# The last four 256-token blocks of a mixture layer as two blocks of 512 tokens, in a planned attention and MoE kernel

## The chip, the cores and the metric

One core of one Trainium2 chip runs the whole kernel. The metric is device time in microseconds (us) of one execution, as the median of several runs. The engines are named as the profile names them: PE is TensorE's matrix products, PEld its loading of the stationary operand, DVE VectorE, ACT ScalarE, POOL GpSimd, SP SyncE, which issues the transfers (DMA).

## The reference: what is computed

Causal attention over 4 sequences of 576 tokens with 8 heads of 64, mixed with a linear memory read by a gate per head; then two dense feed-forward layers, each with inner width 2048, over all 2304 tokens. Cut to what matters:

```python
local = softmax(causal(q @ k.T / 8)) @ v
x = g * mem_out + (1 - g) * local        # 2304 tokens x 512
h = x @ w_in;  x = (h * sigmoid(h)) @ w_out            # first MoE, weights 512x2048 and 2048x512
h = x @ w2_in; out = elu(h) @ w2_out                   # second MoE
```

The weights arrive as float64 and are turned into float32 on the chip.

## The kernel before

**Blocks.** The 2304 tokens are nine blocks of 256: A and B of each of the four sequences (query tiles 0 and 1; and two of the other three), and one block T that gathers the last 64 tokens of each sequence. `order` lists them as (0,A), (0,B), ... (3,B), (T,T), so `order[5]` is (2,B), `order[6:8]` are (3,A) and (3,B), and `order[8]` is T. Attention writes its results to DRAM (`xd`), and `x_load` fetches a block of it.

**First MoE.** `moe1_block` takes one block. For each pair j of 128-row tiles of the inner width it makes h (bank `h` of PSUM, two halves of 256 columns): per tile four slices of the depth, three products each, since every float32 is held as two float32r parts (upper by upper, upper by lower, lower by upper). That is 24 products of 256 columns for a pair. Then ACT takes tanh into `t`, DVE combines it with h, ACT and DVE split it into the two parts `g`, and 24 more products of 256 columns add the pair's share to `acc0` and `acc1`. A whole block has 8 pairs, so 192 + 192 = 384 products. For the first two blocks some pairs use float32 directly, and they are done in two halves; none of that is touched.

**Where it stands.** `interleave` mixes the attention of the later heads with blocks of `moe1` as filler for PE. The list `first` holds the halves of blocks 0 and 1 and `order[2:LAST]`, with LAST = 6, thus blocks 2 to 5. Blocks 6, 7 and T follow.

**Second MoE.** Pairs of its weight tiles are loaded (`w2_fetch`), turned to float32 (`w2_values`: one ACT and three DVE instructions for each of 4 tiles) and made into left operands (`w2_parts`). The raw tiles of pairs 0 and 1 have places of their own (`early`: x21 to x27 and g1, in pool `p2`, which opens when the attention pool is closed); later pairs are loaded into places (`stage`) of first weights that are done with, and so are all finished operands (`home`). Its second products are 512 columns wide already: operand `g` of 128 tokens stationary, 512 columns of the weight moving. Its first products are 256 wide.

**What sets the order.** Nothing runs in the order in which it is written. `Plan` collects all operations, `Plan.cost` gives each one a time, `Plan.schedule` makes a list schedule forwards and backwards four times, and the best one is emitted as a fixed order for every engine. For PE a single product of n columns was costed at

```python
return max(n / (2.4 if once else 0.6) + 2.0, 0.84 * m * (1 if once else 2))
```

nanoseconds, where `once` means float32r. All instructions are recorded through one helper (L194), so the profile's groups are told apart by tiles.

Of the kernel before, what the change touches and what calls it, by code (L numbers as in the profile page):

```python
# [27 lines left out]
AHEAD = 4  # L28
LAST = 6
W1A = 20  # L30
# [21 lines left out]
class View:  # L52
    """A part of a tile, named before the tile has its place on chip."""

# [59 lines left out]
    def box(self):  # L114
        """Partitions and columns that the view can touch (the whole bank in PSUM)."""
        t = self.tile
        if t.space == "psum":
            return (0, 128, 0, 1)
        lo = self.off
        hi = lo + sum(st * (n - 1) for st, n in self.dims)  # L120
        if t.space == "dram":
            return (0, 1, lo, hi + 1)
        w = t.width
        c = [(st, n) for st, n in self.dims if st % w]
        c0 = lo % w
        return (lo // w, hi // w + 1, c0, c0 + sum(st * (n - 1) for st, n in c) + 1)


class LateTile(View):
# [10 lines left out]
    def heads(self):  # L140
        """The operations that no other operation on the tile comes before."""
        users = set(self.users)
        return [o for o in users if not (o.deps & users)]
# [11 lines left out]
class Plan:  # L155
    """Collects the program, orders it by a list schedule over the engines, then emits it."""

# [27 lines left out]
    def add(self, eng, calls):  # L185
        """One operation: an instruction, or a few that an engine takes one after the other."""
        op = Op()
# [39 lines left out]
    def cost(op, fn, args, kw, ins, outs, together):  # L227
# [6 lines left out]
        if op.eng == "PE":  # L234
            if fn == "transpose":
                return max(ins[0].shape[0] / 1.2, 0.84 * cols(ins[0]))
            n, m, once = cols(kw["rhs"]), cols(kw["lhsT"]), kw["rhs"].dtype != F32
            if together > 1:
                return max(55.0, 30 + n / 4.8) if once else max(85.0, 27 + n / 1.2)
            return max(n / (2.4 if once else 0.6) + 2.0, 0.84 * m * (1 if once else 2))  # L240
        if op.eng == "DMA":
# [59 lines left out]
    def schedule(self, back):  # L301
        """List schedule: each engine takes, of what is ready, what comes first in priority.
        Backwards, it goes from the last operation to the first."""
        ops = self.ops
# [56 lines left out]
def attention_moe_moe_kernel(  # L361
# [50 lines left out]
    def mm2(parts):  # L412
        """Products on the two column halves of the array, side by side."""
        op = nc.add("tensor", [("matmul", (o,), dict(lhsT=l, rhs=r, start=start, stop=stop, skip_group_check=True))
                               for o, l, r, start, stop in parts])
        pe[0] += op.cost
# [7 lines left out]
    def split(t, src):  # L424
        """t[:, 0] and t[:, 1]: two float32r parts that add up to src."""
        split2(t[:, 0], t[:, 1], src)
# [33 lines left out]

    # Products that go nowhere, while the tensor engine would wait: they bring its clock up.
    zero = mask[:, 0:128]
# [4 lines left out]

# [1 line left out]
    win, wout = {}, {}  # L469
# [14 lines left out]

    # A float64 arrives as two 32-bit words. Scaling the upper word by 2^-112 as a float32
    # moves the exponent from bias 1023 to bias 127, for either sign; three bits of the lower
    # word complete the float32 significand. The value takes the place of the first half of the words.
    def w_value(raw):
# [41 lines left out]
    def w_again(c, f):  # L530
        """The parts of a weight tile that was used as a whole."""
        v = new(mp, [128, 512], F32, "t", 2)
# [3 lines left out]
    def part(w, i):  # L536
        """The upper (0) or lower (1) float32r part of a weight tile."""
        return w[:, (1 - i) * 512:(2 - i) * 512]

# [1 line left out]
    def x_load(blk):  # L541
        raw = new(mp, [128, 4, 256], F32, "stg", 2)
        b, r = blk
# [96 lines left out]

# [1 line left out]
    # Two heads at a time, which share the partitions: the first has 0..63, the second 64..127.  # L642
    bet = new(at, [128, H], F32, "sm4", 2)
# [16 lines left out]
    def native(task):  # L660
        """Scores from float32 operands, or from float32r parts (two passes, but parts to make)."""
        b, p, rg = task
        return b == 0 and p < (NATA if rg == "A" else NATB)
# [103 lines left out]
    def soft(task, u, nms):  # L767
        """Softmax, times 1 - g, of head u of the pair over the query tiles A (0 and 1) or 2 and 3,
        or of both heads over the last half tile."""
        b, p, rg = task  # L770
# [38 lines left out]
    def spread(t, c, u):  # L809
        """Of 128-column steps from c on, the half that is head u's."""  # L810
        return t[:, c:c + 256].rearrange("p (n h w) -> p n h w", h=2, w=64)[:, :, u, :]

    def a_T(task):
        """Probabilities of the query tiles 0 and 1, keys on the partitions, head by head."""
        res = []
# [10 lines left out]
    def b_T(task, kt):  # L826
        """The same of the query tiles 2, 4 and 3 for one tile of keys; 64 columns of one head are
        followed by 64 of the other."""
        a = new(at, [128, 640], F32, "a", 2)
# [53 lines left out]
    def av_mm(task, av, steps):  # L883
        """Adds to av (heads on either half of the partitions, queries along) for (columns, tile of
        keys, rows, probabilities of a head)."""
        v = pr_t[task]["v"]
# [66 lines left out]
    def merge(T, Sx):  # L953
        """The transposes and products of a pair between the softmax steps of the next one."""
        T, Sx = list(T), list(Sx)
# [85 lines left out]
    def place1(k):  # L1041
        """The places of the last weight tiles serve before those are there."""
        n = 2 * NF - LEND
# [19 lines left out]
    first = [x + (h,) for h in (0, 1) for x in order[:2]] + order[2:LAST]  # L1063
    g = moe1(first, order[LAST])
    calls = [0]
# [8 lines left out]

# [1 line left out]
    # Winograd's form of Strassen's seven products stands for the eight of h by halves: of the depth (k,  # L1076
    # two of its tiles each), of a pair of weight tiles (f) and of the tokens (n). With
    #   s1 = w01 + w11, s2 = s1 - w00, s3 = w01 - w00, s4 = w10 - s2,
    #   t1 = x01 - x00, t2 = x11 - t1, t3 = x01 - x11, t4 = x10 - t2 for w[k][f] and x[k][n]
    # they are w00 x00, w10 x10, s4 x11, w11 t4, s1 t1, s2 t2, s3 t3, and h[f][n] has h00 = p1 + p2,  # L1080
    # h01 = p1 + p6 + p5 + p3, h10 = p1 + p6 + p7 + p4, h11 = p1 + p6 + p7 + p5.
    # The pairs go over the tokens in two sweeps, whose sums meet in DRAM.
    nc.late[p2] = [o for row in nc.tags.values() for t in row if t.pool is at for o in t.users]
# [14 lines left out]

    # Places of the second weights, in the order in which the first ones are done with.
    slots = [f"w{c}_{2 * j + u}" for j in range(NF // 2) for c in range(2) for u in range(2)]  # L1100
# [10 lines left out]
    home["half", 3] = home["half", 0]  # L1111
    early = [(p2, f"x2{i}") for i in range(1, 8)] + [(p2, "g1")]
    w2t, wo2, w2raw, halves = {}, {}, {}, {}

    def w2_fetch(p):
# [3 lines left out]
        for i, (c, f) in enumerate(((0, 2 * p), (0, 2 * p + 1), (1, 2 * p), (1, 2 * p + 1))):  # L1119
            if p < 2:  # L1120
                pl, tag = early[4 * p + i]
                raw = new(pl, [128, 1024], I32, tag, 2 if tag == "g1" else 1)
            else:
# [8 lines left out]
    def w2_parts(p):  # L1132
        """The seven left operands of a pair of weight tiles, and its two tiles of the second product."""
        raws = w2raw.pop(p)
# [40 lines left out]
    def x2_split(raws):  # L1175
        """The right operands."""
        x = [[raw[:, 2 * k:2 * k + 2, :] for raw in raws] for k in range(2)]
# [23 lines left out]
    def product(p, o, wi, x, start, xi=None):  # L1201
        """Adds product wi to o."""
        n = 0
# [5 lines left out]
    def gemm1_2(p, x, nb):  # L1209
        """h, from the products of a pair."""  # L1210
        A, C = bank("s", 2), bank("tp", 2)
# [108 lines left out]
    def w2_steps(n, end):  # L1320
        """Steps of making the second weights, up to those of pair end - 1."""
        for _ in range(n):
# [3 lines left out]

    g = moe1(order[LAST:8], order[8])
    for p in range(2):
        w2_fetch(p)
    vals = [w2_values(p) for p in range(2)]  # L1330
    run(g)
    for p in range(2):
# [8 lines left out]

    run(moe1(order[8:], wnext=wnext))
    for x in parts:
# [81 lines left out]
```

## Time and profile before

| | |
|---|---|
| three runs | 1041.01, 1041.64, 1045.52 us; median 1041.64 us |
| span of the profiled execution | 1046.4 us |
| PE busy in the span | 1028.0 us, 98%, 7206 instructions |
| PEld, DVE, ACT busy | 87%, 68%, 60% |
| granted clock of PE, first 75 us; afterwards | 0.73 to 0.86; 1.00 |

The profiled execution's own span, 1046.4 us, is 4.8 us above the median of the runs. The page's busy time of PE is modelled from pipelined products, so a product's cost is read from starts: the start of one run of equal products to the start of the next, divided by their number.

### The profile page before, as it was taken

How to read it: one execution, taken by the hardware profiler on the slowest of the kernel's cores; microseconds unless marked ns; L12 is line 12 of the kernel's file. 1: busy time of each engine (PE TensorE's matmuls, PEld its weight loads, DVE VectorE, ACT ScalarE, POOL GpSimd, SP SyncE). 2: the span in 40 equal slices, each digit the busy share in tenths (PEclk: the TensorE clock that was granted, in tenths of full speed). 3: DMA queues.
4: the chain of work that ended last, by engine and by line, in shares of the span. 5: the costliest groups of instructions: out<-in, count | busy, mean ns of one | idle time of the engine just before them, and what ended most of it. 6: DMA issues, size and time to landing. Idle time of an engine off the chain costs nothing.

```text
span 1046.4 us, 19128 instructions
## 1 busy us (share of the span) xinstructions
PE 1028.0 (98%) x7206; PEld 913.2 (87%) x7206; DVE 715.5 (68%) x1782; ACT 632.9 (60%) x1434; POOL 9.9 (1%) x54
## 2 busy tenths in 40 slices
PE   7899999999999999999999999999999999999998
PEld 5456887998888888999999999999899899999997
DVE  4979998888777675552223257999969985656554
ACT  5878988989888787422223154766556654434333
POOL 1000000000000000000000000000000000000000
PEclk7889999999999999999999999999999999999999
DMA  8864673452433321601010013434225320302010
GB/s 243 285 168 129 162 228 102 120 168 78 143 98 95 116 86 34 230 10 41 1 41 21 1 42 117 145 105 143 69 91 174 106 100 22 101 22 81 21 61 21
DMA packets 102685, 105.19 MB, mean 101 GB/s; under 512 B 13760, under 2 KB 84928, under 8 KB 102592
## 3 DMA queue, kind: packets, MB, share of 16 engines
q1 hardware_dynamic: 102592, 103.97, 32.5%
q8 instruction: 56, 0.92, 0.4%
q14 instruction: 37, 0.30, 0.1%
HBM read 84.02 MB, written 19.92 MB: 99 GB/s over the span
## 4 chain that ended last, share of the span: by engine, by line
PE 94%; DVE 2%; DMA 2%; SPq 1%; issue 0%; ACT 0%; DVEq 0%
PE acc L194 31%; PE h L194 24%; PE s L194 16%; PE tp L194 13%; PE av L194 10%; SPq L194 1%; DVE w L194 1%; DMA w<-in_moe_w_out 1%; DMA kl<-in_kT 1%; DMA zb<-in_z_prev 0%; DVE e L194 0%; DVE qm L194 0%; DVE eA L194 0%; DVE sm L194 0%; DVE nm L194 0%
## 5 line engine op out<-in xcount | busy, mean ns | idle before, releaser
L194 PE MATMUL h<-x,w 128*128 128x256 f32 x1632 | 223.3, 286 | 0.0
L194 PE MATMUL acc<-g,w 128*128 128x256 f32 x1536 | 210.8, 286 | 0.0
L194 PEld LDWEIGHTS h<-x,w 128*128 128x128 f32 x1632 | 206.2, 191 | 1.9 <-issue 0.8
L194 PEld LDWEIGHTS acc<-g,w 128*128 128x128 f32 x1536 | 194.3, 191 | 0.9 <-issue 0.2
L194 PE MATMUL acc<-w,g 128*128 128x512 f32 x480 | 131.1, 392 | 0.0
L194 PE MATMUL s<-x,w 128*128 128x256 f32 x864 | 126.4, 282 | 0.0
L194 PEld LDWEIGHTS s<-x,w 128*128 128x128 f32 x864 | 118.3, 190 | 5.8
L194 DVE SCALAR_TENSOR_TENSOR t<-t,h 128x512 f32<-128x512 f32 x72 | 49.3, 685 | 107.9 <-ACT t L194 107.7
L194 ACT ACTIVATE e<-e,sm 128x512 f32<-128x512 f32 (+2 forms) x160 | 107.1, 687 | 14.8 <-DVE sm L194 14.6
L194 ACT ACTIVATE t<-h 128x512 f32<-128x512 f32 x72 | 43.0, 597 | 113.0 <-PE h L194 112.6
L194 PEld LDWEIGHTS acc<-w,g 128*128 128x128 f32 x480 | 85.8, 189 | 13.6
L194 PE MATMUL tp<-x,w 128*128 128x256 f32 x672 | 96.6, 282 | 0.0
L194 PEld LDWEIGHTS tp<-x,w 128*128 128x128 f32 x672 | 90.2, 190 | 3.4
L194 ACT COPY a<-tp 128x384 f32<-128x384 f32 (+2 forms) x160 | 65.1, 426 | 27.5 <-PE tp L194 21.0
L194 DVE SCALAR_TENSOR_TENSOR w<-w 128x512 int32<-128x512 int32 x108 | 72.4, 684 | 0.8 <-ACT w L194 0.3
L194 ACT ACTIVATE e<-h 128x512 f32<-128x512 f32 (+1 forms) x80 | 47.1, 590 | 39.4 <-DVE h L194 38.7
L194 DVE TENSOR_TENSOR g<-e,g 128x512 fp32r<-128x512 f32 (+1 forms) x80 | 50.5, 635 | 22.1 <-ACT g L194 21.1
L194 ACT CAST g<-e 128x512 fp32r<-128x512 f32 (+1 forms) x80 | 46.1, 578 | 26.1 <-DVE e L194 25.6
L194 DVE TENSOR_TENSOR g<-t,g 128x512 fp32r<-128x512 f32 x64 | 44.0, 688 | 24.3 <-ACT g L194 24.2
L194 DVE TENSOR_TENSOR x<-stg,x 128x256 fp32r<-128x256 f32 (+2 forms) x86 | 46.0, 550 | 20.4 <-ACT x L194 20.0
L194 PE MATMUL tp<-ident,e 128*128 128x128 f32 (+1 forms) x304 | 55.5, 280 | 4.4 <-ACT a L194 3.5
L194 PE MATMUL av<-a,vr 128*64 128x320 f32 (+4 forms) x448 | 59.1, 385 | 0.0
(137 smaller groups left out, 1611.2 us busy)
## 6 DMA issues: line engine op xcount, KB each, us to landing
w<-in_moe_w_in SPq DMA_DIRECT2D x27, 512.0 KB, 5.0
w<-in_moe_w_out SPq DMA_DIRECT2D x27, 512.0 KB, 4.7
raw<-in_kT SPq DMA_DIRECT2D x48, 144.0 KB, 2.9
y<-y SPq DMA_DIRECT2D x18, 256.0 KB, 2.6
qm<-in_qn SPq DMA_DIRECT2D x32, 128.0 KB, 2.4
vr<-in_vn SPq DMA_DIRECT2D x16, 256.0 KB, 2.9
raw<-in_qT SPq DMA_DIRECT2D x24, 144.0 KB, 3.1
raw<-in_qT SPq DMA_DIRECT2D x24, 128.0 KB, 2.7
```

The source lines that it names most:

```text
L194: r = getattr(issue, fn)(*[a.make() if isinstance(a, View) else a for a in args], **{k: v.make() if isinstance(v, View) else v for k, v in ...
```

## The change

`moe1_wide` takes two blocks at once: h of one tile of the inner width is one product chain of 512 columns into a bank of its own (two banks `s` and two banks `tp` in turn), `g` holds 512 tokens, and four whole banks (`acc0`, `acc1`, `h`, `av`) collect the result. It is called for blocks 6 and 7, and then for blocks 5 and T. LAST falls to 5, so block 5 is no longer among the filler of attention. The raw tiles of the second weights of pair 1 lose their own places and go to `stage`; pair 0 keeps four (x25, x26, x27, h2), the first two of which first hold the raw x of blocks 6 and 7. The cost that the planner puts on a product rises from n/2.4 + 2.0 to n/2.4 + 13.5 ns, which moves the whole order, attention included. The rest of the diff takes out comments.

```diff
-LAST = 6
+LAST = 5
...
-            return max(n / (2.4 if once else 0.6) + 2.0, 0.84 * m * (1 if once else 2))
+            return max(n / (2.4 if once else 0.6) + (13.5 if once else 3.0), 0.84 * m * (1 if once else 2))
...
+    def moe1_wide(blks, tags=(), wnext=None):
+        with nc.ahead(XHP):
+            raws = [x_load(blk, new(p2, [128, 4, 256], F32, tags[i]) if tags else None) for i, blk in enumerate(blks)]
+            x = []
+            for k in range(2):
+                hi, lo = [new(p2, [128, 2, 512], F32R, f"x2{2 * k + i + 1}") for i in range(2)]
+                for i, raw in enumerate(raws):
+                    c = slice(256 * i, 256 * i + 256)
+                    split2(hi[:, :, c], lo[:, :, c], raw[:, 2 * k:2 * k + 2, :])
+                x.append((hi, lo))
+        acc = [bank(tg) for tg in ("acc0", "acc1", "h", "av")]
+        g_t = {}
+
+        def gemm1(f):
+            h = bank(("s", "tp")[f % 2], 2)
+            w, n = win[f], 0
+            for kt in range(4):
+                c = slice(kt * 128, (kt + 1) * 128)
+                for wi, xi in ((0, 0), (0, 1), (1, 0)):
+                    mm(h[:], part(w, wi)[:, c], x[kt // 2][xi][:, kt % 2, :], n == 0, n == 11)
+                    n += 1
+            t = new(mp, [128, 512], F32, "t", 2)
+            g_t[f] = new(*((mp, [128, 2, 512], F32R, "g"), (p2, [128, 2, 512], F32R, "g1"))[f % 2], 2)
+            with nc.ahead(HP):
+                nc.scalar.activation(t[:], h[:], AF.Tanh, scale=0.5)
+                nc.vector.scalar_tensor_tensor(out=t[:], in0=t[:], scalar=1.0, in1=h[:], op0=ALU.add, op1=ALU.mult)
+                split(g_t[f], t[:])
+
+        def gemm2(f):
+            g, w = g_t.pop(f), wout[f]
+            for dm in range(4):
+                c = slice(dm * 128, (dm + 1) * 128)
+                for n, (wi, gi) in enumerate(((0, 0), (1, 0), (0, 1))):
+                    mm(acc[dm][:], part(w, wi)[:, c], g[:, gi, :], f == 0 and n == 0, f == NF - 1 and n == 2)
+
+        for f in range(NF + 2):
+            if f < NF:
+                gemm1(f)
+            if f > 1:
+                gemm2(f - 2)
+                if wnext is not None and f % 2:
+                    wnext(f // 2 - 1)
...
-    g = moe1(first, order[LAST])
+    g = moe1(first)
...
-    early = [(p2, f"x2{i}") for i in range(1, 8)] + [(p2, "g1")]
+    early = [(p2, t) for t in ("x25", "x26", "x27", "h2")]
...
-            if p < 2:
-                pl, tag = early[4 * p + i]
-                raw = new(pl, [128, 1024], I32, tag, 2 if tag == "g1" else 1)
+            if p == 0:
+                pl, tag = early[i]
+                raw = new(pl, [128, 1024], I32, tag)
...
-    g = moe1(order[LAST:8], order[8])
+    moe1_wide(order[6:8], ("x25", "x26"))
...
-    run(moe1(order[8:], wnext=wnext))
+    moe1_wide([order[5], order[8]], wnext=wnext)
```

What the planner made of it, at three places. In these names x is the split input (of narrow and wide blocks alike), w any weight tile (numbers cut short: w_10 is the tile of the tenth slice), g the split middle result.

TensorE in the first MoE after attention, one round before: the first products of two tiles for 256 tokens, then their second products.

```order
L194 MATMUL h_5840<-x_6_5705,w_2_1_2345 128x256 x3
L194 MATMUL h_5840<-x_6_5727,w_2_1_2345 128x256 x3
L194 MATMUL h_5840<-x_6_5731,w_2_1_2345 128x256 x3
L194 MATMUL h_5840<-x_6_5745,w_2_1_2345 128x256 x3
L194 MATMUL h_5840<-x_6_5705,w_3_1_2427 128x256 x3
L194 MATMUL h_5840<-x_6_5727,w_3_1_2427 128x256 x3
L194 MATMUL h_5840<-x_6_5731,w_3_1_2427 128x256 x3
L194 MATMUL h_5840<-x_6_5745,w_3_1_2427 128x256 x3
L194 MATMUL acc_8_5874<-g_5843,w_0_1_2677 128x256 x6
L194 MATMUL acc_8_5884<-g_5843,w_0_1_2677 128x256 x6
```

The same engine now, in the wide block of (3,A) and (3,B): the end of one tile's first products, then a tile's second products into four banks.

```order
L194 MATMUL s_6336<-x_0_5733,w_2_1_2366 128x512
L194 MATMUL s_6336<-x_0_5751,w_2_1_2366 128x512
L194 MATMUL s_6336<-x_0_5733,w_2_1_2366 128x512 x2
L194 MATMUL s_6336<-x_0_5751,w_2_1_2366 128x512
L194 MATMUL s_6336<-x_0_5733,w_2_1_2366 128x512
L194 MATMUL acc_9_6356<-g_6313,w_0_1_2648 128x512 x3
L194 MATMUL acc_9_6363<-g_6313,w_0_1_2648 128x512 x3
L194 MATMUL h_6369<-g_6313,w_0_1_2648 128x512 x3
L194 MATMUL av_6375<-g_6313,w_0_1_2648 128x512 x3
```

A product of width 512 stands where two of width 256 stood, and a tile's second products go to four banks instead of two.

TensorE at the end of attention before: the last products of the last heads (av), inside block (1,B) of the first MoE.

```order
L194 MATMUL acc_7_4862<-g_5628,w_13_0_1710 128x256 x5
L194 MATMUL av_5681<-a_5691,vr_5210 64x320 x2
L194 MATMUL av_5681<-a_5719,vr_5210 64x192 x2
L194 MATMUL av_5681<-a_5719,vr_5210 64x64 x2
L194 MATMUL av_5681<-pt_5712,ms_5543 128x320
L194 MATMUL acc_7_4862<-g_5628,w_13_0_1710 128x256
```

The same place now:

```order
L194 MATMUL h_5587<-x_5_4741,w_10_0_1354 128x256 x2
L194 MATMUL av_5544<-a_5556,vr_5075 64x320 x2
L194 MATMUL av_5544<-a_5585,vr_5075 64x192 x2
L194 MATMUL av_5544<-a_5585,vr_5075 64x64 x2
L194 MATMUL av_5544<-pt_5580,ms_5410 128x320
L194 MATMUL h_5587<-x_5_4741,w_10_0_1354 128x256
```

Attention now ends at the first products of tile 10 of that block, where before it ended at the second products of tile 13: counted over the whole order, 1184 products of the first MoE stand ahead of the last av row, 1313 before.

SyncE's transfers in the first microseconds before: the third pair of q and k (kh, kl) right behind the first two weight tiles.

```order
L194 DMA raw_161<-in_qT 64x576 x2
L194 DMA w_0_0_170<-in_moe_w_in 128x4x256
L194 DMA w_0_0_191<-in_moe_w_out 128x1024
L194 DMA kh_213<-in_qT 128x256
L194 DMA kl_223<-in_kT 128x256
```

And now:

```order
L194 DMA raw_163<-in_qT 64x576 x2
L194 DMA w_0_0_172<-in_moe_w_in 128x4x256
L194 DMA w_0_0_187<-in_moe_w_out 128x1024
L194 DMA zb_214<-in_z_prev 128x128
L194 DMA w_14_0_217<-in_moe_w_in 128x4x256
L194 DMA kh_246<-in_qT 128x256
L194 DMA kl_255<-in_kT 128x256
```

A small load and a third weight tile of 512 KB now stand ahead of that pair.

## Rows read from the trace of the kernel before

**Rows 1.** The page's head and its part 1: busy time, share, instructions.

```profile
span 1046.4 us, 19128 instructions
PE 1028.0 (98%) x7206; PEld 913.2 (87%) x7206; DVE 715.5 (68%) x1782; ACT 632.9 (60%) x1434; POOL 9.9 (1%) x54
```

**Rows 2.** Stretch, length; busy us (count) of PE, PEld, DVE, ACT, POOL; clock; DMA; GB/s.

```profile
0.00:25.00 25.00, 17.96 (x106) 12.13 (x107) 12.79 (x64) 13.46 (x40) 2.63 (x14) 0.73 0.83 249
25.00:50.00 25.00, 22.24 (x113) 11.89 (x111) 23.09 (x87) 21.32 (x58) 0.80 (x3) 0.86 0.86 278
...
75.00:175.00 100.00, 99.06 (x598) 75.63 (x596) 94.62 (x284) 87.24 (x217) 1.75 (x10) 1.00 0.55 158
175.00:250.00 75.00, 75.00 (x594) 67.07 (x593) 61.47 (x177) 68.29 (x167) 1.23 (x7) 1.00 0.45 130
250.00:425.00 175.00, 175.00 (x1363) 153.70 (x1362) 120.27 (x389) 140.35 (x352) 3.27 (x19) 1.00 0.31 91
...
450.00:625.00 175.00, 175.00 (x1461) 175.00 (x1460) 55.87 (x94) 49.66 (x92) 0.00 (x0) 1.00 0.08 22
...
700.00:850.00 150.00, 150.00 (x945) 135.83 (x944) 134.43 (x273) 94.53 (x192) 0.00 (x0) 1.00 0.33 108
```

**Rows 3.** Timeline of TensorE in the first MoE: start us, us, what, count.

```profile
434.77 3.04 PE L194 MATMUL acc<-g,w 128*128 128x256 f32 x24
437.65 3.04 PE L194 MATMUL h<-x,w 128*128 128x256 f32 x24
```

**Rows 4.** Timeline of TensorE in the second MoE, products 512 wide.

```profile
754.96 1.55 PE L194 MATMUL acc<-w,g 128*128 128x512 f32 x6
756.35 0.84 PE L194 MATMUL h<-w,g 128*128 128x512 f32 x3
...
1020.17 2.91 PE L194 MATMUL acc<-w,g 128*128 128x512 f32 x12
1022.91 1.12 PE L194 MATMUL tp<-x,w 128*128 128x256 f32 x8
...
1035.61 5.86 PE L194 MATMUL acc<-w,g 128*128 128x512 f32 x25
```

**Rows 5.** Groups of instructions of DVE and ACT: busy us, mean ns.

```profile
L194 DVE SCALAR_TENSOR_TENSOR w<-w 128x512 int32<-128x512 int32 x108 | 72.4, 684 | 0.8 <-ACT w L194 0.3
L194 DVE SCALAR_TENSOR_TENSOR t<-t,h 128x512 f32<-128x512 f32 x72 | 49.3, 685 | 107.9 <-ACT t L194 107.7
...
L194 DVE TENSOR_TENSOR g<-t,g 128x512 fp32r<-128x512 f32 x64 | 44.0, 688 | 24.3 <-ACT g L194 24.2
...
L194 ACT ACTIVATE t<-h 128x512 f32<-128x512 f32 x72 | 43.0, 597 | 113.0 <-PE h L194 112.6
...
L194 ACT CAST g<-t 128x512 fp32r<-128x512 f32 x64 | 39.6, 619 | 20.6 <-DVE t L194 20.6
...
L194 DVE TENSOR_SCALAR w<-w 128x512 int32<-128x512 int32 x54 | 22.3, 421 | 0.1
...
L194 DVE TENSOR_TENSOR h<-x,x 128x256 f32<-128x256 f32 x32 | 13.5, 421 | 8.9 <-ACT x L194 8.7
```

**Rows 6.** Timeline of all engines in the first 16 us.

```profile
8.47 0.51 SPq L194 DMA_DIRECT2D w<-in_moe_w_out  x1
...
9.50 0.61 SPq L194 DMA_DIRECT2D kl<-in_kT  x1
...
15.84 0.55 PE L194 MATMUL s<-kl,kh 64*128 64x128 f32 x1 [2.37 <-DMA kl<-in_kT]
```

**Rows 7.** Timeline at the end of attention.

```profile
424.67 0.81 PE L194 MATMUL av<-pt,ms 128*128 128x320 f32 x2
...
425.96 0.32 SPq L194 DMA_DIRECT2D xdB<-xt  x1
```

**Rows 8.** The page's part 6: KB of one load, us from issue to landing.

```profile
w<-in_moe_w_in SPq DMA_DIRECT2D x27, 512.0 KB, 5.0
```

**Rows 9.** Waits of TensorE from 75 to 430 us: total, times, longest.

```profile
PE tp L194 <- ACT a L194: 0.9, 1, 0.9
```

More of the change, by code (lines that the diff above doesn't have):

```diff
@@ L538, in part, with x_load @@
         return w[:, (1 - i) * 512:(2 - i) * 512]
-    def x_load(blk):
-        raw = new(mp, [128, 4, 256], F32, "stg", 2)
+    def x_load(blk, raw=None):
+        if raw is None:
+            raw = new(mp, [128, 4, 256], F32, "stg", 2)
         b, r = blk
@@ L639, in moe1_block @@
         nc.sync.dma_start(x2d[blk].rearrange("k p n -> p k n"), ev[:])
+    def moe1_wide(blks, tags=(), wnext=None):
[37 more added lines that the diff above has]
+                    wnext(f // 2 - 1)
+        for dm in range(4):
+            ev = new(mp, [128, 512], F32, "t", 2)
+            nc.scalar.activation(ev[:], acc[dm][:], AF.Copy, scale=0.5)
+            for i, blk in enumerate(blks):
+                nc.sync.dma_start(x2d[blk][dm], ev[:, 256 * i:256 * i + 256])
     bet = new(at, [128, H], F32, "sm4", 2)
@@ L1330, in attention_moe_moe_kernel @@
     vals = [w2_values(p) for p in range(2)]
-    run(g)
     for p in range(2):
```

## The prediction, made before the changed kernel was run

> **What bounds the kernel now.** I read the page's head first: PE is busy for 1028.0 of 1046.4 us [rows 1]. Since that busy time is modelled, the stretches come next. From 75 us on PE is busy for the whole of nearly every stretch at a granted clock of 1.00, the full 2.4 GHz, while DVE and ACT change from light to heavy [rows 2]. In the stretch of the last narrow blocks, 450 to 625 us, PE and PEld are both busy for 175 of 175 us, DVE for 56 and ACT for 50: nothing but the stream of products sets the pace there. In 700 to 850 us, the second MoE, DVE is busy for 134.4 of 150 us and PE still has no gap. Only the first 75 us are different: PE has 18 and 22 of 25 us, at clocks of 0.73 and 0.86, with the DMA engines busy for 83% and 86%. So a change after 425 us is worth what it takes off the stream of products, as long as it makes no new wait.
>
> **The products, the main term.** The timeline of the narrow stage starts 24 products at 434.77 us and the next 24 at 437.65 us [rows 3]: 2.88 us, 120.0 ns for 256 columns. The columns alone take 256 / 2.4 = 106.7 ns at that clock, which leaves 13.3 ns for each product. Four blocks of 384 are 1536 products, 1536 x 120.0 ns = 184.3 us. The change makes 768 of 512 columns. The first MoE has none today, but the second has, and its timeline gives three prices [rows 4]: six from 754.96 to 756.35 us, 231.7 ns each, with DVE heavily loaded; twelve from 1020.17 to 1022.91 us, 228.3 ns; and the last 25, 5.86 us with the last product's own 0.39 us in it, so 24 starts in 5.47 us, 227.9 ns. I take 228.3 ns, since DVE and ACT are light in the first MoE too: 768 x 228.3 = 175.3 us. **The term is -9.0 us.** Its ends: at 231.7 ns 177.9 us, -6.4; and if exactly half of the 13.3 ns goes away for every old product, 768 x 13.3 ns, -10.2.
>
> **Around the wide products, nothing.** Tanh, combining, cast and subtraction work on 128x512 before and after: 0.597 + 0.685 + 0.619 + 0.688 = 2.6 us in a chain [rows 5], 16 of them for two blocks as before. The chain of one tile is covered by 12 products of the next tile, 12 of the one after, and two sets of second products, 4 x 12 x 228.3 ns = 11.0 us; the narrow block has two sets of 24 x 120 ns, 5.8 us. If the chain came 8 us late in one place, PE would still not see it. The wide x of blocks (3,A) and (3,B) must come through DRAM from the last heads. In the order, 184 narrow products stand between the last av product and the end of the narrow round that precedes the first wide one, 22.1 us. The store is issued 1.3 us after the start of the last av product [rows 7], and even three transfers of 5.0 us each, the time of a 512 KB load [rows 8], with two pairs of cast and subtraction behind them are 1.3 + 15.0 + 2.6 = 18.9 us. Without that cover, if the wide block came first, it would be a gap of that size. Between the two wide blocks, and between the second one and the second MoE, 36 second products of 228.3 ns, 8.2 us, run while the next inputs are split: two casts and two subtractions of 512, 2.6 us, before the first of them is needed. I cost both seams at nothing.
>
> **The second weights.** Pair 1 loses its early place: its raw tiles wait for tiles 5 to 7 of the first weights, which are free only after about 11 of 32 sets of twelve in the last wide block, at 30 us of 88 us. Behind that, the order puts on DVE, up to the block's end, the values of 10 raw tiles (10 x (0.421 + 2 x 0.684) = 17.9 us), 9 steps of the block (9 x (0.685 + 0.688) = 12.4 us), 15 subtractions of full and 10 of half width (15 x 0.688 + 10 x 0.421 = 14.5 us): 44.8 us [rows 5]. It has from 30 + 5.0 us (the load) to about 84.5 us, 49.6 us, so it is loaded to 90%. The stretch of 700 to 850 us has DVE at the same 90% and PE without a gap [rows 2]. I take 0 and keep +3 as the upper end, one tile's values and one chain late at the last seam. It can't gain, because PE does not wait there today.
>
> **The start.** The third pair of q and k now stands behind one more small load and one more weight of 512 KB. Before, its key load was issued at 9.50 us, 1.03 us after the last weight's, and PE waited 2.37 us for it until 15.84 us [rows 6]. Two more issues of about 0.5 us and 512 KB at the 249 GB/s of that stretch [rows 2], 2.1 us, make it 3.1 us late. A part is made up later: in 25 to 50 us DVE is busy for 23.1 of 25 us, so the weight tile that came early saves something there. The bounds are -1.0 (two issue slots saved later) and +3.1; I take **+1.0**.
>
> **Attention with less filler.** The planner now charges a product what the trace shows, so it packs fewer among the softmax steps: 1313 - 1184 = 129 products, 129 x 120 ns = 15.5 us, go behind the end of attention. From 75 to 430 us PE waited 0.9 us that the profile can name [rows 9], so attention should simply end 15.5 us earlier and the work follow later: 0 net. In 175 to 250 us ACT is busy for 68.3 of 75 us (91%), in 250 to 425 us for 140.4 of 175 us (80%) [rows 2]. Squeezed by 15.5 us over these 250 us, ACT comes to (208.7 - 129/48 x 1.2) / 234.5 = 88%: short of full, with local waits possible. I take 0, and for the range -1 to +3.
>
> **The sum.** Against the profiled execution, 1046.4 - 9.0 + 0 + 0 + 1.0 + 0 = 1038.4 us of span. That execution lies 4.8 us above the median of the runs, so on the scale of the median it is 1041.6 - 8.0 = **1033.6 us**.
>
> **The rivals.**
> First, **the saving isn't there**: the 120.0 ns is a cost by columns, and a wide product takes twice as long, 240 ns. Then only the start is left, 1041.6 + 1.0 = 1042.6 us. For it speaks that PEld is busy all the time in the narrow stage and may set 120 ns itself; against it that 512 columns take 228 ns in this kernel [rows 4]. Chance 0.06. The Trainium skill ("TensorE: Matmul & The Clock Gate", section "Wait — 56ns, not 53.3ns?") states that warm back-to-back products cost their columns at 2.4 GHz plus about 2.5 ns; by that, 768 products saved would be an estimated 1.9 us, and the result no measurable change. The trace disagrees, with 13.3 ns beyond the columns at width 256 and 14.6 to 18.4 ns at width 512.
>
> Second, **small waits eat half**: the start costs its 3.1, the last seam its 3, and the products go at 231.7 ns: 1041.6 - 6.4 + 6.1 = 1041.3 us. For it: DVE at 90% at the seam and the longer DMA queue. Against it: all three would have to go wrong. With milder mixtures, chance 0.18.
>
> Third, **slower: ACT becomes the bound of attention.** If the softmax steps of 75 to 425 us can't come faster than they do, attention does not shorten, PE stands idle where the 129 products were, and they are paid again behind it: 1041.6 - 8.0 + 15.5 = 1049.1 us. It decides from the point where ACT, or the chain of one pair of heads, fills the shortened stretch; 91% in 175 to 250 us speaks for it, and the missing waits of PE [rows 9] and 80% later speak against it. Chance 0.06. That the change doesn't do what it says is no case here: the order shows the wide products.
>
> **How the numbers follow.** The forecast has 0.70, the rivals 0.06, 0.18 and 0.06. Half a per cent, about what a measurement of this kernel can tell from no change, is 5.2 us: faster means below 1036.4 us. The low end: -10.2 - 1.0 - 1 gives 1029.4; I put it at 1029.5. Upwards the single costs reach 1041.3 us, the second rival at its worst; the milder half of it lies under 1040, so 1040 as the high end leaves out the first and the third rival and a small part of the second, under 2 in 10. Of the forecast's 0.70 I keep 0.68 as faster, and the rest of the cases give 0.26 for within and 0.06 for slower.
>
> **What would show it.** PE instructions 6438 instead of 7206. Runs of 12 wide products between starts 2.74 us apart; 5.5 us for each tile of a wide block; no idle PE between 425 us and the end. Attention's last av product near 410 us instead of 425. First product on the third pair of keys at 16 to 19 us. Wrong would be: wide products at 235 ns or more, PE waiting for ACT in attention, a gap before or behind a wide block, or PE waiting for DVE as the second MoE begins.

## The result, and the profile after

The changed kernel takes 1030.6 us (median of four executions, 1030.1 to 1032.9), the kernel before 1042.7 us beside it (1041.0 to 1045.5): a ratio of 0.9884, 95% interval 0.9858 to 0.9911. Two views answer to the ones read before. First the page's head and part 1, as in [rows 1]:

```profile
span 1028.4 us, 17616 instructions
...
PE 1012.0 (98%) x6438; PEld 869.7 (85%) x6438; DVE 716.8 (70%) x1774; ACT 630.0 (61%) x1426; POOL 10.0 (1%) x54
```

The share of PE is what it was; it has 768 instructions fewer and the span is 18.0 us shorter. Then the stretches behind attention, with the columns of [rows 2]:

```profile
402.00:450.00 48.00, 48.00 (x391) 47.50 (x390) 22.94 (x40) 17.04 (x31) 0.00 (x0) 1.00 0.30 92
450.00:625.00 175.00, 175.00 (x852) 148.35 (x851) 76.01 (x125) 61.65 (x105) 0.00 (x0) 1.00 0.17 51
...
700.00:850.00 150.00, 150.00 (x949) 136.03 (x948) 126.99 (x257) 89.68 (x182) 0.00 (x0) 1.00 0.35 113
```

PE is still the whole of every stretch, but PEld has fallen from 175.00 to 148.35 us in 450 to 625 us: 851 loads there instead of 1460, since a wide product has one load where two narrow ones had two. What TensorE waited for from 75 us to the end is one line (total, times, longest):

```profile
PE tp L194 <- ACT a L194: 0.4, 1, 0.4
```

So there is no gap around the wide blocks. Their pace stands in the timeline of TensorE (start us, us, what, count):

```profile
478.47 2.88 PE L194 MATMUL tp<-x,w 128*128 128x512 f32 x12
481.19 1.52 PE L194 MATMUL acc<-g,w 128*128 128x512 f32 x6
482.55 0.84 PE L194 MATMUL h<-g,w 128*128 128x512 f32 x3
483.23 0.84 PE L194 MATMUL av<-g,w 128*128 128x512 f32 x3
483.91 2.88 PE L194 MATMUL s<-x,w 128*128 128x512 f32 x12
```

From start to start, twelve products take 2.72 us, 226.7 ns each, and a tile of a wide block takes 5.44 us. The columns alone are 512 / 2.4 = 213.3 ns, which leaves 13.4 ns; at 256 columns it was 13.3 ns [rows 3]. So 768 x (2 x 120.0 - 226.7) = 10.2 us are gone, the end of the prediction's product term that it called "exactly".

But the two profiled spans differ by 18.0 us. Where attention ends divides them. The rows list the products of the last heads in the window of 380 to 450 us (count, shortest / median / longest ns, first and last start). Here and below, attention "ends" at the start of its last such product. Before:

```profile
L194 PE MATMUL av<-pt,ms x10: 377/432/537, 380.5 to 425.0; 128*128 128x320 f32 x6, 128*128 128x256 f32 x4
```

After:

```profile
L194 PE MATMUL av<-pt,ms x6: 377/432/537, 383.9 to 402.0; 128*128 128x320 f32 x4, 128*128 128x256 f32 x2
```

Attention ends 23.0 us earlier, and 15.5 us of that are the 129 products that now stand behind it. The other 7.5 us were gained before that point, and the change was to give nothing there. Whether it did was the question of the experiments: **theory**, the width is the whole gain, 10.2 us, and the 7.5 us belong to these two executions; **rival**, the new order of the start is worth something of its own.

### The profile page after: what moved, and what is told of

It reads as the page before. It is cut to its first block, busy times and chain, and to the rows that moved or that the text cites. A ratio compares the mean times of both kernels' runs of the same rounds, so it can differ in the third digit from the quotient of the medians.

```text
span 1028.4 us, 17616 instructions
## 1 busy us (share of the span) xinstructions
PE 1012.0 (98%) x6438; PEld 869.7 (85%) x6438; DVE 716.8 (70%) x1774; ACT 630.0 (61%) x1426; POOL 10.0 (1%) x54
## 4 chain that ended last, share of the span: by engine, by line
PE 94%; DMA 2%; ACT 1%; DVE 1%; SPq 0%; issue 0%; DVEq 0%; ACTq 0%
PE acc L194 27%; PE s L194 20%; PE h L194 17%; PE tp L194 17%; PE av L194 13%; DMA kl<-in_kT 1%; DMA w<-in_moe_w_in 1%; SPq L194 0%; DMA w<-in_moe_w_out 0%; ACT e L194 0%; DVE w L194 0%; DMA sm<-in_beta 0%; ACT w L194 0%; ACT a L194 0%; DVE qm L194 0%
## 5 line engine op out<-in xcount | busy, mean ns | idle before, releaser
L194 PE MATMUL s<-x,w 128*128 128x256 f32 (+1 forms) x1056 | 173.9, 302 | 0.0
L194 PEld LDWEIGHTS s<-x,w 128*128 128x128 f32 x1056 | 155.6, 190 | 14.0
L194 PE MATMUL acc<-g,w 128*128 128x256 f32 (+1 forms) x960 | 156.8, 307 | 0.0
L194 PEld LDWEIGHTS acc<-g,w 128*128 128x128 f32 x960 | 134.4, 190 | 8.1
L194 PE MATMUL tp<-x,w 128*128 128x256 f32 (+1 forms) x864 | 140.7, 306 | 0.0
L194 PEld LDWEIGHTS tp<-x,w 128*128 128x128 f32 x864 | 124.1, 190 | 9.6
L194 PE MATMUL h<-x,w 128*128 128x256 f32 x864 | 129.1, 291 | 0.0
L194 ACT ACTIVATE e<-e,sm 128x512 f32<-128x512 f32 (+2 forms) x160 | 106.8, 690 | 15.5 <-DVE sm L194 14.8
L194 PEld LDWEIGHTS h<-x,w 128*128 128x128 f32 x864 | 112.7, 191 | 2.2 <-issue 0.7
L194 DVE TENSOR_TENSOR g<-e,g 128x512 fp32r<-128x512 f32 (+1 forms) x80 | 50.7, 636 | 21.3 <-ACT g L194 20.1
L194 PE MATMUL av<-w,g 128*128 128x512 f32 x192 | 58.4, 392 | 0.0
L194 PE MATMUL h<-w,g 128*128 128x512 f32 x192 | 56.6, 391 | 0.0
```

Of the source, the lines that this page charges most:

```text
L194: r = getattr(issue, fn)(*[a.make() if isinstance(a, View) else a for a in args], **{k: v.make() if isinstance(v, View) else v for k, v in ...
```

## The experiments

**Width undone.** The changed kernel with every wide product issued as two of 256 columns, in the same places and with the same cost for the planner, so that DVE, ACT and the transfers keep their order.

```diff
+        def mmw(o, l, r, start, stop):
+            op = nc.add("tensor", [("matmul", (o[:, 256 * u:256 * u + 256],), dict(
+                lhsT=l, rhs=r[:, 256 * u:256 * u + 256], start=start and u == 0, stop=stop, skip_group_check=True))
+                for u in range(2)])
+            op.cost = 512 / 2.4 + 13.5
...
```

Both kinds of wide product, into h and into the four banks, then go through `mmw`.

> The changed kernel with every wide product issued as two products of 256 columns, in the same order on every engine; only the width is undone. Theory (a fixed cost of about 13.3 ns for each product, whatever its width): 768 more products, +10.2 us on the changed kernel, about 1040.8 us, and about 120 ns from start to start of each half. Rival (most of the 12 us came from the new order of the start and of attention): the time stays near 1031 to 1034 us.

Measured: 1044.4 us, ratio 1.0019 (0.9990 to 1.0049). The whole gain is gone, although the new order, the four banks and the freed places are all still there. The time is also 3.6 us above the 1040.8 expected, which was counted from the four first executions of the changed kernel; what lies behind that is seen below. The timeline of TensorE shows 24 products of 256 columns in 2.88 us, the old price:

```profile
480.67 3.04 PE L194 MATMUL tp<-x,w 128*128 128x256 f32 x24
483.55 1.72 PE L194 MATMUL s<-x,w 128*128 128x256 f32 x13
```

**The planner's new cost alone.** The kernel before with only the cost line of the change. The start of all engines, third pair of q and k included, stands as in the changed kernel.

```diff
-            return max(n / (2.4 if once else 0.6) + 2.0, 0.84 * m * (1 if once else 2))
+            return max(n / (2.4 if once else 0.6) + (13.5 if once else 3.0), 0.84 * m * (1 if once else 2))
```

> The kernel before with only the planner's cost of a product changed (n/2.4 + 13.5 ns), all blocks narrow. Theory (products carry the gain, the new order brings the rest of 12.1 - 10.2 us): about 1040.8 us, 2 us under the kernel before. Rival (the order is the larger part): 1035 us or less. It could also be slower if ACT holds attention up with less filler: 1050 us or more.

Measured: 1043.2 us, ratio 0.9992 (0.9960 to 1.0024). The new order is worth nothing that shows, and costs nothing that shows; the interval leaves room for 4.2 us gained or 2.5 us lost, so the 2 us of the theory are neither seen nor excluded.

**The old cost in the changed kernel.** The same line turned back, everything else as changed.

> The changed kernel with the planner's old cost (n/2.4 + 2.0 ns): wide blocks, but the start and attention ordered as the old cost does it, with the start's transfers in the old order. Theory: 10.2 us under the kernel before, 1032.5 us. Rival (the order is the larger part): 1037 us or more.

Measured: 1033.5 us, ratio 0.9906 (0.9877 to 0.9935), 9.8 us less than before. With the start in its old order, the width alone brings the 10.2 us of the sum, within the interval.

**The clock of the start, held up.** In the first 75 us the granted clock was lower in the profile of before than in that of after. The kernel before has 0.73 and 0.86 in the first two thirds [rows 2] and in the third

```profile
50.00:75.00 25.00, 22.26 (x90) 12.76 (x91) 18.29 (x52) 18.50 (x45) 0.21 (x1) 0.80 0.61 174
```

The changed kernel has 0.85, 0.94 and 1.00:

```profile
0.00:25.00 25.00, 18.72 (x114) 12.58 (x114) 14.09 (x66) 14.32 (x41) 2.63 (x14) 0.85 0.81 243
25.00:50.00 25.00, 21.38 (x111) 10.92 (x110) 23.91 (x89) 22.69 (x60) 0.65 (x3) 0.94 0.96 311
50.00:75.00 25.00, 23.56 (x116) 11.82 (x117) 22.95 (x68) 22.04 (x55) 0.41 (x2) 1.00 0.64 180
```

So the kernel before got two products that go nowhere (nothing reads their result) ahead of each TensorE instruction between the last planned product of that kind and the first product of the first MoE, 106 in all.

```diff
+        first_h = min(seq.index(o) for o in nc.tags["h"][1].users)
+        last_fill = max(i for i, o in enumerate(seq) if o.fill)
...
+            if o.eng == "PE" and last_fill < i < first_h:
+                for _ in range(2):
+                    tc.nc.tensor.matmul(idle[:, 0:128].make(), lhsT=zero.make(), rhs=zero.make(), start=True, stop=True,
+                                        skip_group_check=True)
```

> The kernel before with 106 more products that go nowhere, two ahead of each PE instruction between about 27 us and the first product of the first MoE at 61 us, nothing else moved. Theory (before lost time because the granted clock fell to half at 42 to 66 us, which the changed kernel's start avoids): the clock stays at 1.00 there and the time falls by 2 to 5 us, to 1038 to 1041 us. Rival (transfers and DVE set the pace there, and the clock costs nothing): within 1 us of the kernel before, or up to 5.7 us slower, 106 x 0.054 us.

Measured: 1047.1 us, ratio 1.0030 (1.0002 to 1.0058). In the profiled execution the clock did hold; these are two stretches, columns as in [rows 2]:

```profile
20.00:30.00 10.00, 8.42 (x67) 5.70 (x67) 8.49 (x39) 7.10 (x22) 0.25 (x1) 1.00 0.95 290
...
40.00:50.00 10.00, 8.24 (x84) 5.94 (x81) 9.94 (x26) 9.40 (x21) 0.20 (x1) 1.00 0.99 343
```

That execution was one of the quickest of the ten (1043.4 us, mean clock 0.999); the others went down to a mean of 0.990 and up to 1052.8 us. The products that go nowhere cost more than they won, and by the mean clocks of the other executions did not hold the clock every time. The theory of a cure failed: 2 to 5 us less were expected. That the low clock costs time is seen below.

**The changed kernel again.** More executions, since four are few.

> The changed kernel once more, with more executions. The kernel before was measured at 1043.6 us over 29 executions that reach from 1039.0 to 1049.9 us, and the changed kernel at 1030.6 us over only four. Theory A, products only: what stays is 768 products saved at the 13.3 ns beyond their columns, 10.2 us, so over many executions the changed kernel lies 10.2 us below the kernel before of the same job (1033.4 us, if that one is at 1043.6 again), and scatters by as much as that one does (about 1029 to 1038 us). The 12 to 13 us between the first medians are then a lucky draw of the start's clock. Theory B, a start that is better as well: the changed kernel stays 12 to 13 us below, at about 1030.6 to 1031.5 us, and its executions lie within 3 us of each other.

Measured: 1030.0 us (1029.0 to 1037.3) beside 1042.1 us, ratio 0.9896 (0.9869 to 0.9923), that is 10.8 us less with an interval of 8.0 to 13.7. Theory A's 10.2 lies in the middle of it, B's 12 to 13 inside it too. One of the six executions is at 1037.3 us, which B did not expect; the other five lie within 1.6 us of each other, which it did. This run alone does not settle it.

**Half the dose.** Only the second products (into the four banks) as two of 256.

```diff
-                    mm(acc[dm][:], part(w, wi)[:, c], g[:, gi, :], f == 0 and n == 0, f == NF - 1 and n == 2)
+                    mmw(acc[dm], part(w, wi)[:, c], g[:, gi, :], f == 0 and n == 0, f == NF - 1 and n == 2)
```

> The changed kernel, with only the second products of the two wide blocks (384 of 768) issued as two products of 256 columns each, the planned order of all engines unchanged. Dose: if the gain is the cost beyond the columns of each product, half of it goes, 384 x 13.3 ns = 5.1 us more than the changed kernel (about 5.1 us below the kernel before). If the gain hangs on something that the wide blocks share (four banks, the order, the freed queue), it keeps more or loses all. The same kernel also asks why 512-column products cost 228 to 232 ns in the second MoE and 226.7 ns in the wide blocks. Theory switch: the first few wide products behind a run of 256-column ones are longer, some 28 ns in total, so here the 12 first products of each tile, which now stand behind 24 narrow ones, take 12 x 226.7 + 28 ns = 2.75 us, 229.0 ns in the mean, with DVE as light as it was; the time is then another 32 x 0.028 = 0.9 us longer, less what the first narrow products behind wide ones give back. Theory DVE load (as the prediction had it, that a busy DVE makes them longer): they stay at 226.7 ns.

Measured: 1038.2 us, ratio 0.9965 (0.9941 to 0.9989): 3.6 us less than before where 10.2 - 5.1 - 0.6 = 4.5 was due. Its timeline also answers the second question:

```profile
481.35 1.59 PE L194 MATMUL acc<-g,w 128*128 128x256 f32 x12
...
484.22 2.91 PE L194 MATMUL s<-x,w 128*128 128x512 f32 x12
486.97 1.59 PE L194 MATMUL acc<-g,w 128*128 128x256 f32 x12
```

Twelve wide products behind 24 narrow ones take 2.75 us instead of 2.72, 229.2 ns in the mean (229.0 by the starts in whole nanoseconds, against 226.7), and the 24 narrow ones behind them 2.87 instead of 2.88. DVE is no busier than before, 50.72 of 150 us:

```profile
450.00:600.00 150.00, 150.00 (x991) 138.22 (x990) 50.72 (x78) 45.16 (x77) 0.00 (x0) 1.00 0.12 36
```

So a run of twelve wide products pays about 28 ns in all, 12 x (229.0 - 226.7), when it follows narrow ones, with DVE as light as here.

**Four products of 128 columns.** As in the first experiment, with four quarters.

> The changed kernel, with each wide product issued as four products of 128 columns, planned order unchanged. It asks for the law behind 120.0 ns at 256 columns and 226.7 ns at 512. Theory fixed cost: every product pays 13.3 ns beyond its columns whatever its width, so one of 128 columns takes 53.3 + 13.3 = 66.7 ns, four of them 266.7 ns, and the kernel is 768 x (266.7 - 226.7) ns = 30.7 us slower than the changed one, 20.5 us slower than the kernel before. Theory weight load: below some width the load of the stationary operand sets the pace (PEld was busy for 175 of 175 us in the narrow stage before), so 256 columns were at that limit already; then four products take 4 x 120 = 480 ns and the kernel is 194 us slower than the changed one. Anything between tells where the load's own time lies.

Measured: 1201.6 us (two executions), ratio 1.1533 (1.1488 to 1.1578). Neither number came out: it is far above the fixed cost's 1063 us, and a set of four takes 447 ns, a little less than the load's 480. The timeline gives the price:

```profile
482.92 2.84 PE L194 MATMUL acc<-g,w 128*128 128x128 f32 x24
485.60 1.50 PE L194 MATMUL h<-g,w 128*128 128x128 f32 x12
486.94 1.50 PE L194 MATMUL av<-g,w 128*128 128x128 f32 x12
488.28 0.94 PE L194 MATMUL tp<-x,w 128*128 128x128 f32 x7
```

24 products take 2.68 us, 111.7 ns each, where columns and fixed cost would be 66.7 ns. Something that does not shrink with the columns sets this pace, and each product has one load of its stationary operand: the load's time is the likely one, but no run gives two products one load, so this is not shown. Such a floor lies 8.3 ns below the 120.0 ns at 256 columns. The Trainium skill ("TensorE: Matmul & The Clock Gate", section "LDWEIGHTS (loading the stationary operand)") puts a load at its columns divided by 1.2 GHz, an estimated 106.7 ns for 128. The 111.7 ns lie near it.

**All runs on one scale.** The time from the end of attention to the end of the span does not scatter. In each profiled execution it is the span less the start of the last av product, read as in the two rows above; the last column is worked out from counts and prices of products alone. (The kernel with the old cost has 17 more narrow products behind attention than the kernel before, counted in its trace with a pair for each wide one.)

| kernel | span, us | attention ends | rest | rest worked out |
|---|---|---|---|---|
| before | 1046.4 | 425.0 | 621.4 | |
| before, clock held up | 1041.6 | 420.2 | 621.4 | 621.4 |
| new cost only | 1041.8 | 404.9 | 636.9 | 621.4 + 129 x 0.120 = 636.9 |
| changed | 1028.4 | 402.0 | 626.4 | 636.9 - 10.2 = 626.7 |
| changed, again | 1027.6 | 400.9 | 626.7 | 626.7 |
| width undone | 1048.8 | 412.2 | 636.6 | 636.9 |
| changed, old cost | 1035.2 | 422.3 | 612.9 | 621.4 - 10.2 + 17 x 0.120 = 613.2 |
| half the dose | 1034.0 | 402.0 | 632.0 | 626.7 + 5.1 + 32 x 0.02 = 632.4 |
| quarters | 1196.6 | 401.4 | 795.2 | 626.7 + 3072 x 0.1117 - 768 x 0.2267 = 795.7 |

Behind attention every run is explained to 0.5 us. What scatters is what comes before, and there the first 66 us. The first ten av products with pt start as follows (rows as above, window from 0); the changed kernel, the same with its width undone, and the kernel before with the new cost only:

```profile
L194 PE MATMUL av<-pt,ms x10: 379/483/793, 19.4 to 54.8; 128*128 128x256 f32 x8, 128*128 128x320 f32 x2
```

```profile
L194 PE MATMUL av<-pt,ms x10: 379/634/797, 18.8 to 66.7; 128*128 128x256 f32 x8, 128*128 128x320 f32 x2
```

```profile
L194 PE MATMUL av<-pt,ms x10: 379/510/796, 20.3 to 59.3; 128*128 128x256 f32 x8, 128*128 128x320 f32 x2
```

These three have the same instructions in the same order up to there on PE, DVE and ACT, and reach the same point at 54.8, 66.7 and 59.3 us. What differs most is the clock. The stretches (columns as in [rows 2]) of the changed kernel:

```profile
15.00:30.00 15.00, 12.93 (x61) 7.93 (x61) 9.60 (x40) 11.07 (x35) 0.44 (x2) 0.66 0.98 302
30.00:45.00 15.00, 13.32 (x59) 5.83 (x59) 14.91 (x61) 13.88 (x38) 0.41 (x2) 1.00 1.00 328
45.00:60.00 15.00, 12.80 (x63) 6.00 (x64) 13.41 (x41) 13.13 (x32) 0.21 (x1) 1.00 0.92 272
```

and with its width undone:

```profile
15.00:30.00 15.00, 10.85 (x62) 6.58 (x62) 11.33 (x48) 11.23 (x35) 0.41 (x2) 0.85 0.97 300
30.00:45.00 15.00, 14.67 (x36) 5.42 (x36) 8.00 (x34) 9.09 (x26) 0.20 (x1) 0.50 0.83 254
45.00:60.00 15.00, 12.98 (x49) 6.26 (x50) 12.32 (x35) 11.23 (x25) 0.20 (x1) 0.73 0.70 211
```

The second one had TensorE at the lower level, 0.50 (1.2 of 2.4 GHz), for all of 30 to 45 us, after a stretch in which PE was idle for 4.15 of 15 us; it did 36 instructions there against 59, and was busy for 14.67 of the 15 us, so its pace at the lower level set the time.

Six kernels have the same instructions in the same order up to the end of attention. Their profiled executions, by mean granted clock over the whole span and end of attention:

| kernel | clock | attention ends |
|---|---|---|
| changed | 0.995 | 402.0 |
| half the dose | 0.995 | 402.0 |
| quarters | 0.995 | 401.4 |
| changed, again | 0.992 | 400.9 |
| new cost only | 0.990 | 404.9 |
| width undone | 0.981 | 412.2 |

The two with the lowest clocks end last. The kernel before, at 0.985, ends attention at 425.0 us, 409.5 without its 129 products; between the last two rows one would read 409.0 for 0.985. So the 7.5 us are about what the lower clock of that execution accounts for, with its old order. This is a comparison of single executions: the kernel with the old cost, at 0.989 and 408.9 us by the same count, lies some 3 us above what one would read there, so a difference of that size between the orders is not excluded by it. Over the executions the start evens out. The means (not medians), less those of the kernel before beside them, and less what the products are worth:

| kernel | executions | mean against before, us | less products | left over |
|---|---|---|---|---|
| width undone | 10 | +1.3 | 0 | +1.3 |
| new cost only | 10 | +0.3 | 0 | +0.3 |
| changed, old cost | 8 | -9.8 | -10.2 | +0.4 |
| changed, first | 4 | -11.9 | -10.2 | -1.7 |
| changed, again | 6 | -11.2 | -10.2 | -1.0 |
| half the dose | 10 | -4.0 | -4.5 | +0.5 |

Executions of one kernel scatter with a standard deviation of about 3 us, so each difference is good to 1 to 1.5 us (one standard error). What is left over has both signs and nothing to speak of in it. The 106 products that go nowhere, counted the same way over ten executions, stand at +3.0.

## Why the prediction was right, and where it was not

**The product term** was the mechanism, and mis-sized: -9.0 us forecast, -10.2 found. The step that failed is the choice of 228.3 ns. The prediction chose among three prices of the second MoE by how busy DVE was; the half dose shows the longer mean with DVE light. With 226.7 ns for a product and 28 ns in all for a run that follows narrow products, runs of 6, 12 and 24, which all follow narrow ones, come to 231.4, 229.0 and 227.9 ns; [rows 4] has 231.7, 228.3 and 227.9. The pattern was readable before: the mean falls with the length of the run. In a wide block, runs of wide products never meet a narrow one, so the limit of a long run was the price to take.

**Around the wide products, 0**: right. TensorE waits for nothing behind attention, and the rest of the span is explained by products alone, so neither the x of the first wide block nor the middle step came late.

**The second weights, 0 with +3 as the upper end**: right at 0. DVE in 700 to 850 us is busy for 126.99 of 150 us (134.43 before), and PE has no gap there.

**The start, +1.0**: the delay was there, its price can't be told. The third pair's key load is issued later, behind one more weight, as this timeline of the changed kernel shows:

```profile
9.53 0.65 SPq L194 DMA_DIRECT2D w<-in_moe_w_in  x1
...
11.14 0.90 SPq L194 DMA_DIRECT2D kl<-in_kT  x1
...
17.81 1.61 PE L194 MATMUL s<-kl,kh 64*128 64x128 f32 x4 [0.91 <-DMA kl<-in_kT]
```

Its first product starts at 17.81 us, inside the forecast 16 to 19, against 15.84 [rows 6]. But the kernel with the new order alone is at 0.9992 of before, within an interval of -4.2 to +2.5 us: the +1.0 neither shows nor is excluded. What was missing is the scatter of the start, which moves the same point by more than ten us from one execution to another; a term of 1 us there was below what these runs can tell.

**Attention with less filler, 0**: right. With the new cost alone, attention ends 20.1 us earlier in its profile, and the 129 products cost 15.5 us behind it to the tenth; the whole is unchanged within the interval. The forecast for the end of attention was near 410 us and it was 402.0; the difference is the 7.5 us by which these two executions differ ahead of that point.

**The rivals.** By columns alone nothing would have been saved: out, by the pace of 226.7 ns and by the first experiment. Its argument, PEld busy for the whole narrow stage, misled: at 128 columns the same loads pass every 111.7 ns, so at 120 ns they were hardly the limit, though the profile showed PEld at 100%. The rule of 2.5 ns beyond the columns, which the prediction quoted from the Trainium skill ("TensorE: Matmul & The Clock Gate", section "Wait — 56ns, not 53.3ns?"), is not what these products do, each with a load of its own: 13.3 and 13.4 ns at two widths. Small waits eating half, and ACT as the bound of attention: no trace shows either.

**The sum.** 1033.6 us was forecast, 1030.6 measured, inside the range. As a change, 8.0 us were forecast and 12.1 measured between the medians, for the kernel before came out at 1042.7 instead of the 1041.6 of the sum. Of the 4.1 us, 1.2 are the product term; the other 2.9 no run pins down: the start's +1.0 may belong to them, and the scatter of four executions covers the rest, so that the median came this far down is in part luck. Taking all 50 executions of the kernel before (mean 1043.1 us), the 10.2 us of the products lead to about 1033. The ten executions of the changed kernel have a mean of 1031.1; against the kernel before beside them 1.3 us are left over, about one and a half standard errors, which these runs do not settle.

## What to carry to other kernels

Where TensorE is busy without a gap, count products as well as columns: here each float32r product, with a load of its own, cost 13.3 ns beyond its columns at 256 and at 512, so half as many products of twice the width save 13.3 ns for each one that goes, as long as no new wait appears. Whether the 13.3 ns belong to the product or to its load stays open, since the two always went together. Take the price of an operation from a run as long as the one it will stand in, and let a gain in the profile of one execution prove itself where nothing scatters, by cutting the span at a point that both kernels share. A planner's cost moved 129 products past the end of attention and was worth nothing that shows; PE was full on both sides of it.

## What the runs showed of the hardware

- A float32r product with its own load of 128 x 128 goes every 111.7 ns at 128 columns, 120.0 at 256, 226.7 at 512: columns at 2.4 GHz plus 13.3 or 13.4 ns at the two larger widths, and 58.4 ns beyond the columns at the smallest. If 111.7 ns is a flat floor, it would meet the other line at an estimated 236 columns, (111.7 - 13.3) x 2.4; no run tried a width between.
- Twelve wide products behind a run of 256-column ones cost about 28 ns more in total; the first narrow ones behind them give some 10 back (2.75 + 2.87 us against 2.72 + 2.88, in rounding).
- The same order of instructions reached the same point between 54.4 (half the dose) and 66.7 us (width undone) in different executions, with a granted clock of 1.00 or of 0.50 in 30 to 45 us. Why the clock falls in one execution and not in another stays open: with 106 more products it held in the one that was profiled, and the mean clock of the other nine was 0.990 to 0.996.
